# Decode attention with a gated feed-forward on one core: one part of the output-projection weights loaded as two DMAs, of 88 and of 40 partitions

## The chip, the core and the metric

The kernel runs on one core of a Trainium2 chip. The metric is the device time of one execution in microseconds. A time is given as the median of several executions. The profile is one execution of its own.

## What is computed

Two rows (batch 2, one new token each) of width 448 are normalised, and two branches are formed from them. Branch A is attention of 16 query heads over 8 key/value heads of width 256, for the last 2048 positions of a cache of 8192, and the output projection `wo`. Branch B is a two-layer feed-forward with a ReLU. The result is `x + A * silu(B)`.

```python
W = min(4096, max(256, Sk // 4))                       # 2048
q = (xn @ wq).reshape(B, Sq, Hq, Dh)                    # 2 x 1 x 16 x 256
scores = einsum("bhqd,bhkd->bhqk", q, k) * (Dh ** -0.5)
p = softmax(scores); o = einsum("bhqk,bhkd->bhqd", p, v)
s = o.reshape(B, Sq, Hq * Dh) @ wo                      # wo: 4096 x 448
g = silu(maximum(xn @ w1, 0) @ w2)
out = x + s * g
```

All inputs are bf16. The keys and values that are read are 32 MB, the weights about 10.5 MB, and `wo` alone 3.5 MB.

## The kernel before

The work is written as lists of operations, one list for each engine, with semaphore waits worked out from each operation's dependencies (`_Prog`, L24 to L159). The order on each engine is the order in which the operations are written.

Attention runs in four turns `u` = 0 to 3, each for one batch row and four key/value heads. A turn's keys (4 MB) go into one of two buffers `kbuf0` and `kbuf1`, its values (4 MB) into `vbuf0`, and the last turn's values into `vbuf1`. In a turn VectorE transposes the keys in four blocks (`do_T`, L376), TensorE forms the scores (`do_S`, L383), VectorE and ScalarE do the softmax (L400), and TensorE multiplies with the values (`do_PV`, L426). Then `attend_scale`, `attend_turn` and `attend_spread` (L443 to L467) bring the turn's result into `at_z`, from which the output projection reads it.

All large loads are issued by SyncE on its one queue, in the order in which they are needed: wq, keys 0, the rest of wq, keys 1, values 0, w1, w2, keys 2, values 1, keys 3, values 2, values 3 in two parts of 48 and 16 positions per partition (L566), and at last `wo` in seven parts. Each load has a semaphore of its own and counts as landed when 16 has been counted on it.

`wo` is laid out so that each of the 128 partitions holds 32 rows of 448 numbers (896 bytes each). A part of `n` rows per partition is one DMA with one piece of `n * 896` bytes for each partition. The parts are `WO_PARTS = [9, 7, 5, 4, 3, 2, 2]` (L191). They go into `kbuf0`, which is free when turn 2's scores are done (the dependency `st["S", 2, NBLK - 1]`). The loop that issues them is:

```python
for n in WO_PARTS:
    v, j = divmod(j0, NWO)
    d_wo[j0] = pr.dma(SP, wo_sb[:, j0 * D:(j0 + n) * D], wo_src[v, :, j * D:(j + n) * D], [st["S", 2, NBLK - 1]])
    j0 += n
```

The last turn ends on TensorE in this order (L574 to L610): a loop of five times two matmuls without use for the result (`idle_loop(5, 2)`, L574), the products with values 3 (the first three quarters wait for the first part of values 3, the last quarter for the second part), the spreading of turn 2's and turn 3's results, and the output projection `do_wo`. That is written in two pieces. Rows `j` = 0 to 8 (the first part of `wo`) are nine matmuls of 448 columns into `obk`. Their four column groups are added up by way of `sums` with eight more matmuls. Rows 9 to 31 are four matmuls of 112 columns each, 92 in all, into `hbk`. The first matmul of rows 9, 16, 21, 25, 28 and 30 waits for the part of `wo` that begins there (`d_wo.get(j)`, L590). After the 92 matmuls VectorE multiplies with the gate (L611), adds `x` (L613), and ScalarE issues the store of 8 x 112 numbers (L615).

Of the kernel before, what the change touches and what calls it, by code (L numbers as in the profile page):

```python
# [11 lines left out]
PE, DVE, ACTE, SP, POOL = "pe", "dve", "act", "sp", "pool"  # L12
# [149 lines left out]
def bass_recurrent_scan__sliding_block_cached__dense_activation_relu__decode_kernel(  # L162
# [11 lines left out]
    B, Sq, D = A_x.shape  # L174
# [11 lines left out]
    NBLK = DH // 64  # L186
# [6 lines left out]
    NWO = 16  # L193
# [5 lines left out]
    with es:  # L199
        pr = _Prog(nc, es)  # L200

        def named(name, shape, dt):
            return es.enter_context(nc.sbuf_tensor(name, shape, dt))
# [4 lines left out]
        def view(t, off, dims, n=128, p0=0, pstep=1):  # L208
            width = t.shape[1]
            return bass.AP(t, p0 * width + off, [[width * pstep, n]] + dims)  # L210
# [45 lines left out]
        at_z = named("at_z", [128, 32 * GAP], BF)  # L256
# [24 lines left out]
        wq_sb, w1_sb, w2_sb, wo_sb = vbuf[1], wf, wf, kbuf[0]  # L281
# [4 lines left out]
        wo_src = A_wo.rearrange("(v p j) n -> v p (j n)", v=2, j=NWO)  # L286
        assert SLOTS * HC <= UW and 32 * D <= UW and W2_AT + 14 * D <= UW

        st, d_k, d_v = {}, {}, {}
# [70 lines left out]
        def mm(out_ap, lhsT, rhs, start, stop=False, **kw):  # L360
            return lambda e: e.matmul(out_ap, lhsT=lhsT, rhs=rhs, start=start, stop=stop,  # L361
                                      skip_group_check=True, **kw)
# [134 lines left out]
        def tiled(bank, z, k, w, lo, first, last, deps):  # L497
            g = k % 4
            return pr.op(PE, mm(view(bank, 0, [[1, D]], n=2, p0=32 * g), view(z, k * GAP + 3, [[4, 2]]), w[:, lo:lo + D],
                                k < first, k >= last, tile_position=(0, 32 * g)), deps)  # L500
# [66 lines left out]
        d_wo, j0 = {}, 0  # L567
        for n in WO_PARTS:
            v, j = divmod(j0, NWO)
            d_wo[j0] = pr.dma(SP, wo_sb[:, j0 * D:(j0 + n) * D], wo_src[v, :, j * D:(j + n) * D], [st["S", 2, NBLK - 1]])  # L570
            j0 += n
        turn(3)
        v_f = pr.op(DVE, lambda e: e.tensor_copy(sums[:, :], view(fbk, 0, [[1, D]])), [st["F"]])
# [13 lines left out]
        def do_wo(lo, hi):  # L587
            o = None
            for j in range(lo, hi):
                deps = [d_wo.get(j), st["at_z", 2 + j // NWO]]  # L590
                if j < TILED:
                    o = tiled(obk, at_z, j, wo_sb, j * D, 4, TILED - 4, deps)
                    continue
                for i in range(4):
                    lo2 = j * D + i * NCOL
                    o = pr.op(PE, mm(view(hbk, 0, [[1, NCOL]], n=NROW), at_z[:, j * GAP + 3 - i:j * GAP + 3 - i + NROW],
                                     wo_sb[:, lo2:lo2 + NCOL], False, j == 2 * NWO - 1 and i == 3), deps)
                    deps = []
            return o

        attend_spread(3)
        m_t = do_wo(0, TILED)
        v_w = pr.op(DVE, lambda e: e.tensor_copy(sums[:, :], view(obk, 0, [[1, D]])), [m_t, m_f])
        idle_work(3)
# [3 lines left out]
        v_g = pr.op(DVE, lambda e: e.tensor_tensor(out=g_sb[:, :], in0=g_ap, in1=tmp[:, :], op=ALU.mult), [v_rc])  # L608
        fold_tiles(view(hbk, 0, [[1, NCOL]], n=NROW), True, False, [v_w])
        m_o = do_wo(TILED, 2 * NWO)  # L610
        v_t = pr.op(DVE, lambda e: e.tensor_tensor(  # L611
            out=tmp[:, :], in0=hbk[0:NROW, 0:NCOL], in1=g_sb[:, :], op=ALU.mult), [m_o, v_g])
# [33 lines left out]
```

## Time and profile before

| | us |
|---|---|
| time, median of 5 runs | 111.08 |
| lowest and highest of the 5 | 110.92 and 113.09 |
| time of the profiled execution | 112.69 |
| span in its profile | 111.2 |

The span is what lies between the first and the last instruction of the profile. The profiled execution's time is 1.49 us more than that. It is one execution, and it was 1.61 us longer than the median.

The DMA engines moved 44.13 MB in it, at a mean of 397 GB/s. VectorE was busy for 62.9 us and TensorE for 60.7 us.

A page gives busy time by engine, the span in 40 slices, the DMA queues, the chain of work that ended last, the costliest groups of instructions and the DMA issues. The trace also keeps for each load the sixteen times at which its semaphore was counted up by a DMA engine. Where such times are given, they are in us from the start of the span.

### The profile page before, as it was taken

What the parts mean: (1) busy time and instruction counts of PE and PEld (TensorE: products, weight loads), DVE (VectorE), ACT (ScalarE), POOL (GpSimd) and SP (SyncE); (2) the same over time, 40 slices, a digit from 0 to 9 for tenths busy, and PEclk for the clock granted to TensorE, in tenths of its full rate; (3) what the DMA queues carried; (4) which work ended last, traced back from release to release, by engine and by line L of the source; (5) the groups of instructions that cost most, each with busy time, mean ns of one, the idle gap of its engine ahead of it and who ended that gap; (6) DMA issues with size and microseconds to landing.
All of it is one profiled execution on the core that took longest, in us unless ns stands there. A gap on an engine that the chain in (4) does not pass through costs nothing. (4 is left out here: it accounts for less than half of the span.)

```text
span 111.2 us, 1362 instructions
## 1 busy us (share of the span) xinstructions
PE 60.7 (55%) x552; PEld 19.6 (18%) x558; DVE 62.9 (57%) x96; ACT 10.2 (9%) x19; POOL 3.1 (3%) x11
## 2 busy tenths in 40 slices
PE   0001000085699132999555788940078894798993
PEld 0000000030110020002141010220001033325692
DVE  1249009995200479992578998335699733615601
ACT  4990000000000200000200000020000002000000
POOL 7300000000000000000000000000000000000000
PEclk9999999999999975599985557999557999679999
DMA  3989989998998999999989999999999998999900
GB/s 65 490 383 495 448 351 464 482 401 377 530 412 377 424 419 392 415 447 542 401 365 436 460 412 389 495 412 412 448 448 424 395 433 383 420 414 407 376 25 1
DMA packets 3045, 44.13 MB, mean 397 GB/s; under 512 B 354, under 2 KB 612, under 8 KB 1508
## 3 DMA queue, kind: packets, MB, share of 16 engines
q1 hardware_dynamic: 3008, 44.11, 93.7%
q8 instruction: 1, 0.02, 0.1%
q10 hardware_dynamic: 36, 0.01, 0.0%
HBM read 44.11 MB, written 0.00 MB: 397 GB/s over the span
## 5 line engine op out<-in xcount | busy, mean ns | idle before, releaser
L379 DVE STREAM_TRANSPOSE kt<-kbuf 128x2048 f32<-128x2048 f32 x16 | 35.9, 2286 | 8.0 <-DMA kbuf<-in_A_k_cache_dram 8.0
L361 PE MATMUL sbk<-kt,qz 128*8 128x512 bf16 x128 | 31.0, 1070 | 13.7 <-PEq L102 13.6
L401 DVE TENSOR_REDUCE rm<-sbk 128x1 f32<-128x512 f32 x4 | 2.8, 691 | 14.5 <-PE sbk L361 14.5
L361 PE MATMUL obk<-vbuf,xr 128*4 128x512 bf16 x28 | 3.2, 627 | 13.9 <-DMA vbuf<-in_A_wq_dram 13.9
L407 ACT ACTIVATE et<-sbk,bias 128x512 bf16<-128x512 f32 x4 | 2.7, 687 | 81.1 <-DVE bias L405 81.1
L361 PEld LDWEIGHTS sbk<-kt,qz 128*8 128x8 bf16 x128 | 2.4, 87 | 29.1 <-issue 28.9
L361 PE MATMUL pbk<-et,spread 128*128 128x32 bf16 x64 | 2.6, 193 | 7.2 <-PEq L102 7.2
L361 PE MATMUL wbk<-q_n,ident 128*128 128x512 bf16 x9 | 4.5, 515 | 2.5 <-DVE qz L396 1.3
L361 PE MATMUL obk<-vbuf,pt 128*16 128x512 bf16 x96 | 5.8, 381 | 0.0
L361 PE MATMUL mbk<-ident,xg 2*128 2x2 bf16 x7 | 0.3, 163 | 8.5 <-DVE xg L325 8.5
L409 DVE STREAM_TRANSPOSE et<-et 128x512 bf16<-128x512 bf16 x4 | 2.8, 711 | 3.4 <-ACT et L407 3.4
L361 PE MATMUL hbk<-kbuf,at_z 128*8 128x112 bf16 x92 | 4.7, 213 | 0.0
L417 DVE TENSOR_TENSOR pt<-pbk,hmask 128x512 bf16<-128x512 f32 x4 | 2.8, 692 | 3.3 <-PE pbk L361 3.3
L361 PEld LDWEIGHTS hbk<-kbuf,at_z 128*8 128x8 bf16 x92 | 4.6, 87 | 0.0
L361 PEld LDWEIGHTS pbk<-et,spread 128*128 128x128 bf16 x64 | 2.2, 99 | 10.4 <-issue 10.4
L361 PEld LDWEIGHTS obk<-vbuf,pt 128*16 128x16 bf16 x96 | 2.5, 94 | 6.8 <-issue 4.7
L361 PEld LDWEIGHTS obk<-vbuf,xr 128*4 128x4 bf16 x28 | 0.8, 115 | 15.4 <-issue 15.4
L456 DVE TENSOR_TENSOR at_exp<-mbk,qmask 128x128 bf16<-128x128 f32 x4 | 1.2, 292 | 4.1 <-PE mbk L361 4.1
L611 DVE TENSOR_TENSOR tmp<-hbk,g_sb 8x112 f32<-8x112 f32 x1 | 0.3, 262 | 4.3 <-PE hbk L361 4.3
L361 PE MATMUL fbk<-wf,h_z 128*2 128x448 bf16 x14 | 1.7, 565 | 1.7 <-DVE h_z L494 1.7
L361 PE MATMUL obk_last<-vbuf,pt 128*16 128x512 bf16 x32 | 2.4, 400 | 0.0
L361 PEld LDWEIGHTS wbk<-q_n,ident 128*128 128x128 bf16 x15 | 1.5, 116 | 4.5 <-issue 2.2
(80 smaller groups left out, 44.8 us busy)
## 6 DMA issues: line engine op xcount, KB each, us to landing
kbuf<-in_A_k_cache_dram SPq DMA_DIRECT2D x4, 4096.0 KB, 23.5
vbuf<-in_A_v_cache_dram SPq DMA_DIRECT2D x3, 4096.0 KB, 15.8
wf<-in_B_w_dram SPq DMA_DIRECT2D x2, 1568.0 KB, 43.0
vbuf<-in_A_v_cache_dram SPq DMA_DIRECT2D x1, 3072.0 KB, 22.5
vbuf<-in_A_wq_dram SPq DMA_DIRECT2D x1, 2560.0 KB, 20.9
vbuf<-in_A_wq_dram SPq DMA_DIRECT2D x1, 1024.0 KB, 6.1
vbuf<-in_A_v_cache_dram SPq DMA_DIRECT2D x1, 1024.0 KB, 24.4
kbuf<-in_A_wo_dram SPq DMA_DIRECT2D x1, 1008.0 KB, 26.2
```

The lines of the kernel that those rows point to most:

```text
L361: return lambda e: e.matmul(out_ap, lhsT=lhsT, rhs=rhs, start=start, stop=stop, skip_group_check=True, **kw)
L379: st["kt", u, blk] = pr.op(DVE, lambda e: e.transpose(view(dst, 0, [[1, 32 * NT]]), view(src, 32 * blk, [[DH // 2, NT], [1, 32]])), [d_k[u ...
L401: v = pr.op(DVE, lambda e: e.tensor_reduce(out=rm[:, :], in_=sbk[:, :], axis=AX.X, op=ALU.max), [st["S", u, NBLK - 1]])
L407: a = st["exp", u] = pr.op(ACTE, lambda e: e.activation(e_sb, sbk[:, :], ACT.Exp, bias=bias[:, 0:1], accum_out=ssum[:, 0:1]), [v, st.get(( ...
L409: token = pr.op(DVE, lambda e: e.transpose(e_t, e_sb), [a, st.get(("Pt", u - 1))])
L417: st["pt", u] = pr.op(DVE, lambda e: e.tensor_tensor(out=view(pt, 0, [[8, NT], [2, 4], [1, 2]]), in0=view(pbk, 0, [[2, NT], [0, 4], [1, 2] ...
L456: st["at", u] = pr.op(DVE, lambda e: e.tensor_tensor(out=view(at_exp, 0, [[16, 8], [8, 2], [1, 8]]), in0=view(mbk, 136, [[1, 8], [8, 2], [ ...
L611: v_t = pr.op(DVE, lambda e: e.tensor_tensor(out=tmp[:, :], in0=hbk[0:NROW, 0:NCOL], in1=g_sb[:, :], op=ALU.mult), [m_o, v_g])
```

## The change

The part of three rows per partition (`n == 3`, rows 25 to 27) is issued as two DMAs, one after the other on the same queue: partitions 0 to 87, and partitions 88 to 127. [...]The bytes, their places and their place in the order of the queue are the same. Row 25's first matmul waits for both. All other parts are one DMA of 128 partitions as before.

```diff
         for n in WO_PARTS:
             v, j = divmod(j0, NWO)
-            d_wo[j0] = pr.dma(SP, wo_sb[:, j0 * D:(j0 + n) * D], wo_src[v, :, j * D:(j + n) * D], [st["S", 2, NBLK - 1]])
+            d_wo[j0] = []
+            for lo, hi in ((0, 88), (88, 128)) if n == 3 else ((0, 128),):
+                d_wo[j0].append(pr.dma(SP, wo_sb[lo:hi, j0 * D:(j0 + n) * D], wo_src[v, lo:hi, j * D:(j + n) * D],
+                                       [st["S", 2, NBLK - 1]]))
             j0 += n
...
             for j in range(lo, hi):
-                deps = [d_wo.get(j), st["at_z", 2 + j // NWO]]
+                deps = d_wo.get(j, []) + [st["at_z", 2 + j // NWO]]
```

## The prediction, made before the changed kernel ran

> **What bounds the kernel now.** I read the slices first, then the DMA issues, then the chain of waits, then the stages of its end.
>
> ```profile
> PEclk9999999999999975599985557999557999679999
> DMA  3989989998998999999989999999999998999900
> q1 hardware_dynamic: 3008, 44.11, 93.7%
> ```
>
> The DMA engines are busy from the second slice to about 106 us; one queue carries nearly all of it. So the last loads, `wo`, land when the stream ends, and only what follows their landing can be short or long. The query on DMA gives their sizes and the time from issue to landing:
>
> ```profile
> kbuf<-in_A_wo_dram SPq DMA_DIRECT2D x1, 1008.0 KB, 26.2
> ...
> kbuf<-in_A_wo_dram SPq DMA_DIRECT2D x2, 224.0 KB, 27.5
> kbuf<-in_A_wo_dram SPq DMA_DIRECT2D x1, 336.0 KB, 29.4
> ```
>
> The reader is to see that each waits over 25 us, in the queue behind values 2 and 3. The 336 KB part is the one that is changed. The chain of waits, from its last third:
>
> ```profile
> 97.68 0.63 PE wbk L361
> 98.32 1.12 PE obk_last L361 x16
> ...
> 102.55 0.66 PE obk L361 x9
> 103.21 0.16 issue
> 103.36 0.59 PE wbk L361 x2
> 103.96 5.43 PE hbk L361 x100
> 109.39 0.02 issue
> 109.42 0.27 DVE tmp L611
> ```
>
> No transfer stands in it: in this execution TensorE is late by itself. The reason is the clock in the stages (columns: stretch and length, PE, PEld, DVE, ACT and POOL busy, PEclk, DMA share, GB/s):
>
> ```profile
> 93.50:98.30 4.80, 3.71 (x27) 1.98 (x36) 1.94 (x4) 0.00 (x0) 0.00 (x0) 0.68 0.95 395
> 102.45:104.60 2.15, 1.99 (x20) 1.04 (x22) 1.55 (x4) 0.00 (x0) 0.00 (x0) 1.00 1.01 397
> 104.60:109.40 4.80, 4.78 (x95) 4.60 (x92) 0.52 (x2) 0.00 (x0) 0.00 (x0) 1.00 0.24 89
> ```
>
> The clock is half from 95.19 to 98.60 us, which falls on the loop of useless matmuls. Its five rounds of two begin at 94.73; the first took 0.43 us, each later one 0.85 or a little less. The value products follow at 98.32; at full clock the loop would end at 94.73 + 5 x 0.43 = 96.88, 1.44 earlier, and the 0.3 us of value products that fell in the half clock would give some 0.15 more: 1.59 in all. The execution was 1.61 above the median. So I read the median run as this one with TensorE about 1.6 earlier at its end, and there the landings matter.
>
> The trace's landing times, the last of sixteen for each part, and when its first matmul began here (92 matmuls in 104.69 to 109.38 start 0.049 apart, so row j begins at 104.69 + 4 x 0.049 x (j - 9)): row 0, landed 100.94, used 102.48; row 9, 102.88 and 104.69; row 16, 104.30 and 106.07; row 21, 105.42 and 107.05; row 25 (the changed part), 106.24 and 107.84; row 28, 106.82 and 108.43; row 30, 107.39 and 108.82. Each has 1.4 to 1.8 us of slack in this execution and next to none 1.6 us earlier. If only one part set the end, TensorE would end at its landing plus what followed its use here: row 0, 100.94 + 6.90 = 107.84; row 9, 107.57; row 16, 107.61; row 21, 107.75; row 25, 107.78; row 28, 107.77; row 30, 107.39 + 0.56 = 107.95. TensorE alone at full clock: 109.38 - 1.59 = 107.79. The profiled execution's own 112.69 has 3.31 us after 109.38; the median less this is 107.77. Four limits stand within 0.2 us of it.
>
> **What the Trainium skill says.** "DMA: Bandwidth & Descriptors", section "Why a DMA increments its semaphore by 16 and not by 1": a load issued by SyncE or ScalarE uses the largest count up to 16 that divides its partitions, the lowest-numbered ones, and the remaining counts are written at once. So 88 gives 11 and 40 gives 10. The trace agrees for 8: the load of `x_c` (8 partitions) shows one count at 1.78, standing for those written at once, and eight from 5.46 to 5.77. The same page, section "The descriptor swizzle", has a load of 128 partitions give each engine the rows of one SBUF port. "SBUF — State Buffer", section "Door 1: The DMA port swizzle", says that bandwidth depends on how many of the 16 ports are reached, and that partitions 0 to 63 reach 8 of them. Nothing in the trace of before has many bytes on fewer than 16 engines, so whether 11 engines keep their rate is unseen.
>
> **The change part by part.** Removed: 8 pieces of 2688 bytes from each of 16 engines. Added: 8 on engines 1 to 11 and 4 more on 1 to 10. Net: first ten +4, the eleventh 0, the last five -8. The price of one is from the distance of the last landings of rows 21 and 25: (106.24 - 105.42) / 8 = 0.103 us. So the first ten are later by 0.41 and the last five earlier by 0.82, from this part to the end of the queue.
>
> Whether that helps depends on who is last. The sixteen counts of row 30's part lie: eight from 105.82 to 105.99, seven from 106.10 to 106.83, one at 107.39. The same shape is in every load since keys 3, and the one straggler since the first: wq's first part has fifteen from 5.25 to 5.71 and one at 6.88. `x_c`, queued beside that part, was through on all of its eight engines by 5.77, so the straggler is not one of the first eight. Of the other eight, five are relieved, one is unchanged, two are burdened. I take it to be relieved. Then it counts at 107.39 - 0.82 = 106.57; the seven, if among the first ten, at most at 106.83 + 0.41 = 107.24. The last landing is between 106.57 and 107.24, so 0.15 to 0.82 earlier, for rows 28 and 30; row 25's two loads are both in by 106.09 at the latest.
>
> What it is worth: row 30's limit falls from 107.95 to 107.80 or below, and row 0's, 107.84, which the change doesn't touch, is next, with TensorE's own 107.79 behind it. Gain 107.95 - 107.84 = 0.11 us. In an execution like the profiled one the gain is 0.
>
> Other items. One more issue on SyncE: 0.43 us (the median of the `wo` issues), and two issues of the seven are held up by the queue (the last from 82.01 to 89.27). Behind it only the last two parts are issued, and even if the very last waited until the first part of values 3 has landed (95.99), its turn comes about 106, so it costs nothing; that cover of 10 us would have to go first. One more wait at row 25's first matmul: nothing stands between two instructions but the 0.02 to 0.05 us gaps of the chain, so 0 to 0.05, with 28 matmuls and the two VectorE operations behind it; hidden, since the two loads land before TensorE gets there. The other operations are the same in number and order on each engine. Sum on the profiled execution: 112.69 - 0.00; on the median: 111.08 - 0.11 = 110.97, so **111.0**.
>
> Unknown from both sides is the rate of the two loads. Below: at the rate of before, the above. Above: partitions 0 to 63 reach 8 ports, and if each engine takes 8 partitions in a row, engines 1 to 4 and 5 to 8 go to the same ports in pairs. Halved rate adds 0.82 for the load of 88 and 0 to 0.41 for that of 40: with the 0.41 of above, 1.23 to 1.64 on those engines. I take the lower value, since every other packet keeps its rate in this trace, and keep the upper for the range.
>
> **Rivals.** (1) Slower: the burdened engines become the last. Place: those of the first ten that are among the seven late ones; price: 1.23 to 1.64 by halved rate; it decides once the shift exceeds 107.39 - 106.83 = 0.56. Row 30 then lands at 106.83 + 1.23 = 108.06, up to 108.47: later by 0.67 to 1.08, so 111.75 to 112.16; I put 111.8. For it: the port rule above. Against: the eight early engines would have to shift by 1.40 before they matter. (2) Faster: row 30 alone sets the end in the unprofiled runs, and the limits of row 0 and of TensorE are lower there by more than I read. The gain is the landing's, up to 0.82; with 0.65 it is 110.4. For it: row 30's limit is the highest in my list. Against: the distance between row 0 and row 30 is set by one stream, and both shift together. (3) The straggler is the ninth or tenth engine: 107.39 + 0.41, so 111.08 + 0.41 = 111.5. (4) The split doesn't confine the loads to these engines: nothing changes, 111.1.
>
> **How the numbers follow.** The forecast 0.42, rival 3 0.10, rival 4 0.03: these lie within 0.5% (110.52 to 111.64), which is about what a measurement of this kernel can tell from no change. Rival 1 0.28, rival 2 0.17. So same 0.55, slower 0.28, faster 0.17. The range goes from 110.4, rival 2's value, to 111.9, which takes in the lower half of rival 1. The forecast's own range is 110.7 to 111.5.
>
> **What would show it.** Right: the straggler's counts of rows 25 to 31 come 0.4 to 0.8 earlier against those of row 21, and the chain of waits still has no transfer or has row 0's. Five counts of row 25's first load and six of its second come at once. Wrong: the distance from row 21's last landing to row 30's grows beyond 1.97 (107.39 - 105.42), or pieces of 2688 bytes that take well over 0.1 us (rival 1); an end that follows row 30's landing one for one (rival 2).

## The result, and the profile after

The changed kernel took 112.9 us (median of 42 runs). The kernel before, run beside it, took 111.67 us (79 runs, the five of the first table among them). The ratio is 1.0105, with a 95% interval of 1.0087 to 1.0123: slower by about 1.2 us.

The two profiled executions have spans of 110.8 us (after) and 111.2 us (before), and these can't be set against each other. In the one of before, the clock of TensorE was half during the loop of useless matmuls, in this one it was full. What can be compared is the order of events at the end. The slices of the changed kernel, TensorE's clock and the DMA engines:

```profile
PEclk9999999999999955579996569587555999999999
DMA  4989989998998999999999999899999999999960
```

The clock is full from slice 32 on. The DMA engines stay at nine tenths up to slice 38, as before; in slice 39 they are busy for six tenths, where before they were done. The issues, from the query on DMA:

```profile
kbuf<-in_A_wo_dram SPq DMA_DIRECT2D x1, 448.0 KB, 29.4
...
kbuf<-in_A_wo_dram SPq DMA_DIRECT2D x1, 231.0 KB
kbuf<-in_A_wo_dram SPq DMA_DIRECT2D x1, 105.0 KB
```

The 336 KB part has become two. The chain of waits of the changed kernel (start, length, what), from where it turns to a transfer:

```profile
77.17 29.42 DMA kbuf<-in_A_wo_dram
106.59 0.04 issue
106.63 2.34 PE hbk L361 x44
108.97 0.02 issue
109.00 0.27 DVE tmp L614
```

A transfer now stands in it. But it is not one of the two new loads. It was issued at 77.17 and has 44 matmuls behind it, so it is the 448 KB part, rows 21 to 24, which the change doesn't touch and which stands ahead of the new loads in the queue. The timeline of TensorE's last stage (start, length, engine, line, operation, tiles; in brackets the wait before it):

```profile
101.00 0.73 PE L361 MATMUL obk<-kbuf,at_z 128*2 128x448 bf16 x9
...
103.21 2.52 PE L361 MATMUL hbk<-kbuf,at_z 128*8 128x112 bf16 x48
...
106.63 2.33 PE L361 MATMUL hbk<-kbuf,at_z 128*8 128x112 bf16 x44 [0.90 <-DMA kbuf<-in_A_wo_dram]
```

The reader is to see that TensorE ran the 48 matmuls of rows 9 to 20 at its pace, and then stood for 0.90 us before row 21. The landing times (the last of all counts of a part, in us from the start of the span) tell where the delay begins. The last two lines are kernels of the experiments below: two loads of 64 partitions, and the part cut along its rows.

```
first row of the part     0       9      16      21      25      28      30
before                100.94  102.88  104.30  105.42  106.24  106.82  107.39
after                 100.95  102.88  104.54  106.59  107.14  107.61  108.18
halves                101.07  103.03  104.86  106.66  107.42  108.00  108.58
by rows, again        100.96  102.93  104.35  105.47  106.35  106.90  107.48
```

Up to row 9 before and after are alike within 0.01 us. Row 16 is 0.24 late, row 21 is 1.17 late, row 30 0.79. Row 21's last count comes at 106.59. All counts of the load of 88 partitions are in by 106.52. If an engine counts its loads in the order of the queue, which is assumed here, the engine that is last on row 21 takes no part in the load of 88: the straggler is one of the last five, and it was relieved, as the prediction took it. It was slowed before the relief came. In the trace's packet records the pieces of 3584 bytes (rows 21 to 24) took at most 0.155 us before and up to 0.309 after; those of 2688 bytes had a median of 0.107 us before and 0.165 after.

### The profile page after: what moved, and what is told of

It reads as the page before. It is cut to its first block, busy times and chain, and to the rows that moved or that the text cites. A ratio compares the mean times of both kernels' runs of the same rounds, so it can differ in the third digit from the quotient of the medians.

```text
span 110.8 us, 1364 instructions
## 1 busy us (share of the span) xinstructions
PE 60.9 (55%) x552; PEld 19.7 (18%) x558; DVE 62.9 (57%) x96; ACT 10.2 (9%) x19; POOL 3.1 (3%) x11
## 5 line engine op out<-in xcount | busy, mean ns | idle before, releaser
L361 PE MATMUL sbk<-kt,qz 128*8 128x512 bf16 x128 | 31.1, 1072 | 13.4 <-PEq L102 13.3
L361 PE MATMUL obk<-vbuf,pt 128*16 128x512 bf16 x96 | 6.6, 420 | 0.0
L361 PE MATMUL wbk<-q_n,ident 128*128 128x512 bf16 x9 | 3.5, 406 | 2.0 <-DVE qz L396 1.4
L444 DVE TENSOR_SCALAR o_sb<-obk,rs 128x512 bf16<-128x512 f32 x3 | 2.2, 730 | 0.0
```

The lines of the kernel that those rows point to most:

```text
L444: st["osb", u] = pr.op(DVE, lambda e: e.tensor_scalar(out=o_sb[:, :], in0=view(out_bank(u), 0, [[1, 512]]), scalar1=rs[:, u:u + 1], scalar ...
```

## The experiments

Theories at this point. *Shared ports*: a load that isn't one of 128 partitions gives each engine several partitions in a row. Two engines then write through one port of SBUF, the on-chip memory of 128 partitions, at a time, both at half rate, and an engine that is still on an earlier part is slowed through its own port too. *Burden*: the first ten engines have four pieces more, and that is all. *Issue and wait*: one more DMA on SyncE and one more wait on TensorE. *Reading side*: the order of the addresses in HBM, the memory that `wo` is read from.

**The split without partitions.** Two rows, then one row, of all 128 partitions.

```diff
-            for lo, hi in ((0, 88), (88, 128)) if n == 3 else ((0, 128),):
+            for a, b in ((0, 2), (2, 3)) if n == 3 else ((0, n),):
...
+                d_wo[j0].append(pr.dma(SP, wo_sb[:, (j0 + a) * D:(j0 + b) * D], wo_src[v, :, (j + a) * D:(j + b) * D],
+                                       [st["S", 2, NBLK - 1]]))
```

> Rows 25 to 27 as two loads of all 128 partitions, of two rows and of one, both waited for at row 25. Same extra issue on SyncE and same extra wait on TensorE as the changed kernel, no change in which engine or partition moves what. If the extra issue or the extra wait costs the time: ratio to before about 1.0105, like the changed kernel. If it is the partition split (shared ports, or more work on the first ten engines, or the reading side): 1.000, within 0.003, and the last landing of row 21's part stays about 1.1 us after row 16's.

Measured: ratio 0.9938 (0.9911 to 0.9966). Row 21's part landed 1.15 us after row 16's. The cost is gone. That it should be faster than before was not expected, so it was run again:

> The two loads of two rows and of one, once more, since the first look gave 0.9938 where 1.000 was expected and nothing in its landings tells why. If that was the luck of where the half-clock stretches fell: 1.000 within 0.004. If finer parts help in themselves: again 0.994.

Measured: 1.0012 (0.997 to 1.0055), so no change that can be told, and the first figure is no gain to rely on. Its landings stand in the table above and are those of the kernel before to 0.11 us. The extra issue and the extra wait cost nothing that shows. The clock was full in its profile from the loop on, as in that of the changed kernel, so these two can be set side by side. The end of its chain of waits:

```profile
75.57 25.39 DMA kbuf<-in_A_wo_dram
100.96 0.04 issue
101.00 0.73 PE obk L361 x9
...
108.12 0.27 DVE tmp L614
```

The last transfer in it is row 0's, and VectorE's multiplication starts at 108.12, where it started at 109.00 in the changed kernel: 0.88 us.

**The same work for every engine.** Two loads of 64 partitions, and two of 80 and 48. All of these counts are multiples of 16. These two kernels and the one with another source were run in the same rounds as the first run by rows, whose median was 111.67 us; theirs are 113.11, 112.73 and 112.91.

```diff
-            for lo, hi in ((0, 88), (88, 128)) if n == 3 else ((0, 128),):
+            for lo, hi in ((0, 64), (64, 128)) if n == 3 else ((0, 128),):
```

> Rows 25 to 27 as two loads of 64 partitions (0 to 63, 64 to 127). Each uses all 16 engines with 4 pieces, so every engine moves as much as before. Theory of shared ports (a load that is not of 128 partitions gives each engine partitions in a row, so that two engines write one port, and each slows whoever else is on that port): 64 partitions lie on 8 ports for 16 engines, pieces of 2688 bytes take about twice 0.107 us, row 21's straggler lands later than 1.1 us after row 16's, ratio 1.006 to 1.013. Theory of the burden (the first ten engines have 4 pieces more): nothing is left of it, ratio 1.000 within 0.003.

Measured: ratio 1.0074 (1.0042 to 1.0106). Each load counted sixteen times, so all engines took part. The median piece of 2688 bytes took 0.160 us, and row 21 landed 1.80 us after row 16 (1.12 before). The chain of waits of this kernel:

```profile
76.44 30.22 DMA kbuf<-in_A_wo_dram
106.66 0.04 issue
106.70 2.50 PE hbk L361 x44
```

It waits at the same place for the same untouched part, though nobody carries more than before.

> Rows 25 to 27 as two loads of 80 and of 48 partitions. Both use all 16 engines, with 5 and with 3 pieces, so every engine moves as much as before, but its partitions do not fall on the borders of ports. Shared ports: slower, ratio 1.004 to 1.013, pieces of 2688 bytes at a median well over 0.107 us. Burden: 1.000 within 0.003.

Measured: ratio 1.0045 (1.0007 to 1.0082), row 21 again 1.80 us after row 16, median piece 0.154 us. Both came as shared ports had it; burden alone can't do it. In both, row 16 landed 1.83 us after row 9 (1.42 before).

**Another source.** The split of 88 and 40, read from one packed stretch.

```diff
+        packed = A_wo[0:384, :].rearrange("(p j) n -> p (j n)", j=3)
...
+                src = wo_src[v, lo:hi, j * D:(j + n) * D] if n != 3 else packed[lo:hi, :]
```

> The split of 88 and 40 as in the changed kernel, but the source of both loads is one packed stretch of 344 KB of wo (the first 384 rows) and not every 32nd row; rows 25 to 27 of the projection are so left out and other rows taken in their place. The written side is the changed kernel's. If the reading side (the pattern of addresses in HBM) costs the time: ratio near 1.000. Shared ports or burden on the writing side: ratio about 1.010, as in the changed kernel, row 21's last landing 1.8 us or more after row 16's.

Measured: ratio 1.0071 (1.004 to 1.0102), row 21 landing 1.99 us after row 16. So the pattern of addresses that is read isn't the cause.

**The loads by themselves.** Seven loads one after the other behind the kernel before, with nothing else on the queue.

```diff
         pr.op(ACTE, None, [d_o])
+        last, N = d_o, NWO * D
+        for lo, hi in ((0, 128), (0, 88), (88, 128), (0, 64), (64, 128), (0, 80), (0, 128)):
+            last = pr.dma(SP, kbuf[1][lo:hi, 0:N], wo_src[0, lo:hi, :], [last])
+        pr.op(SP, None, [last])
```

> The kernel before, and after its output seven loads of wo rows by themselves, each issued when the one before has landed, 14336 bytes for each partition: 128 partitions, 0 to 87, 88 to 127, 0 to 63, 64 to 127, 0 to 79, 128 again. The added loads are no part of the computation; only their own landing times count. Shared ports with partitions in a row for each engine: 128 partitions take about [...]6.3 us; 64 partitions need the same time although each engine has half the pieces (4.3 us of transfer and not 2.1); 0 to 87 takes about twice the 4.3 us of its 8 pieces; 88 to 127 takes up to twice the 2.1 us of its 4. If every engine keeps its rate whatever the partitions (burden): 6.3, 6.3, 4.1, 4.1, 4.1, 4.7, 6.3.

The stages of the first six, from each load's first packet to the end of its last, in the order of the list (stretch and length, busy time by engine, clock, DMA share, GB/s):

```profile
111.37:117.36 5.99, 0.00 (x0) 0.00 (x0) 0.00 (x0) 0.00 (x0) 0.00 (x0) 0.53 0.81 306
118.63:127.32 8.69, 0.00 (x0) 0.00 (x0) 0.00 (x0) 0.00 (x0) 0.00 (x0) 0.50 0.64 144
128.98:133.38 4.40, 0.00 (x0) 0.00 (x0) 0.00 (x0) 0.00 (x0) 0.00 (x0) 0.50 0.57 130
135.26:139.79 4.53, 0.00 (x0) 0.00 (x0) 0.00 (x0) 0.00 (x0) 0.00 (x0) 0.50 0.93 203
141.87:146.45 4.58, 0.00 (x0) 0.00 (x0) 0.00 (x0) 0.00 (x0) 0.00 (x0) 0.50 0.91 197
148.19:153.52 5.33, 0.00 (x0) 0.00 (x0) 0.00 (x0) 0.00 (x0) 0.00 (x0) 0.50 0.91 215
```

The reader is to see that the load of 88 partitions needs 8.69 us for fewer bytes than the 128 partitions moved in 5.99, and that 64 partitions on all 16 engines move 203 and 197 GB/s instead of 306. By the packet records the median piece of 14336 bytes took 535 ns in the first load, 1087 in the load of 88, 1025 in that of 40, 1105 and 1131 in those of 64, and 1007 in that of 80. So a piece took 1.9 to 2.1 times as long in each of these loads, with nothing else on the queue. From one landing to the next the seven took 7.3, 10.4, 5.9, 6.6, 6.6, 7.0 and 7.4 us. A load of 128 took a microsecond more than was written down. A load of 64 took 0.7 us less than one of 128; burden had put it 2.2 us lower, and shared ports at the same time.

How many pairs of engines share a port doesn't explain all of this. If each engine takes partitions in a row, then by the prediction's own map of the ports engines 1 to 8 of the load of 88 are in pairs, and the other three, on partitions 64 to 87, have their ports to themselves. But its packets fall into eleven rows of eight, each packet beginning where one before it ended, and from the third piece on all eleven rows show 0.86 to 1.13 us for a piece. In the load of 80 all sixteen show 0.97 to 1.03 us from the third piece on, and the pairing gives no reason why they should be alike. Divided by the number of engines the rate is much the same in every load cut by partitions, 12.3 to 13.4 GB/s, against 19.1 with 128 partitions. So each engine of such a load is slowed, with or without a partner; why is open.

**Whose port.** Eight loads of 8 partitions each, four apart. They put the same bytes, in the same pieces, by the same first eight engines, either into the partitions that these engines write in a load of 128, or into those of the last eight engines. Which partitions these are follows the section on the swizzle that the prediction cites; no record here names an engine. The diff is that of the first; in the second the list is (64, 65, 66, 67, 96, 97, 98, 99).

```diff
-            d_wo[j0] = pr.dma(SP, wo_sb[:, j0 * D:(j0 + n) * D], wo_src[v, :, j * D:(j + n) * D], [st["S", 2, NBLK - 1]])
+            for p in (0, 1, 2, 3, 32, 33, 34, 35) if n == 3 else (None,):
+                dst, src = wo_sb[:, j0 * D:(j0 + n) * D], wo_src[v, :, j * D:(j + n) * D]
+                if p is not None:
+                    dst, src = wo_sb[p:p + 29:4, j0 * D:(j0 + n) * D], wo_src[v, p:p + 29:4, j * D:(j + n) * D]
```

> Rows 25 to 27 for partitions 0 to 63 alone, as eight loads of 8 partitions, four apart (0, 4, ..., 28; 1, 5, ...; up to 35, 39, ..., 63), so that each of the first eight engines writes the partitions it writes in a load of 128. Partitions 64 to 127 of these rows are not loaded and left out of the result. The last eight engines have 8 pieces less. Shared ports: nobody is slowed; pieces of 2688 bytes stay at about 0.107 us, row 21's last landing 1.1 us after row 16's, as before; ratio 0.994 to 1.003. Theory that any load of fewer partitions or on fewer engines is slow and holds up the others: as the run with other ports.

> The same eight loads as in the run with the engines' own ports, same bytes, pieces and engines, but for partitions 64 to 127 (64, 68, ..., 92; and so on), whose ports are those of the last eight engines; partitions 0 to 63 of rows 25 to 27 are left out of the result. Shared ports: the straggler among the last eight engines is still on rows 16 to 24 and is slowed: row 21's last landing 1.4 to 2.0 us after row 16's, pieces of 2688 bytes well over 0.107 us at the upper end; ratio 0.003 to 0.009 above that of the run with own ports. Otherwise both runs are alike.

Both kernels took much longer by the clock outside: 114.94 and 115.84 us, of which 4.7 and 4.8 us lie outside the span (1.5 in the kernel before). The ratio of the second is 1.0339 (1.0283 to 1.0395), and for the first, whose executions scatter from 111.87 to 116.87 us, none is given. The ratios that were written down were missed, and don't decide anything. So they are compared inside the span, where both profiled executions have the full clock at the end. TensorE's last stage with the engines' own ports:

```profile
101.03 0.73 PE L361 MATMUL obk<-kbuf,at_z 128*2 128x448 bf16 x9
...
103.25 4.69 PE L361 MATMUL hbk<-kbuf,at_z 128*8 128x112 bf16 x92
```

and with the other ports:

```profile
103.19 1.54 PE L361 MATMUL hbk<-kbuf,at_z 128*8 128x112 bf16 x28
104.92 1.15 PE L361 MATMUL hbk<-kbuf,at_z 128*8 128x112 bf16 x20 [0.20 <-DMA kbuf<-in_A_wo_dram]
106.26 2.33 PE L361 MATMUL hbk<-kbuf,at_z 128*8 128x112 bf16 x44 [0.19 <-DMA kbuf<-in_A_wo_dram]
```

With their own ports the 92 matmuls run without a stop from 103.25 to 107.94. With the other ports TensorE waits at row 16 and at row 21, and ends at 108.59, 0.65 later. Row 16 landed at 104.34 against 104.88, row 21 at 105.47 against 106.21. From row 9's landing to row 21's it is 2.53 us (2.54 before) against 3.36: 0.83 more, which is 8 pieces at 0.103 us, as if the straggler's port had to take the other engine's eight pieces in between. The pieces of 2688 bytes took 0.107 us against 0.189 at the median, and those of rows 21 to 24, which neither kernel changes, at most 0.155 against 0.292. The figure that was written down, row 21 at 1.4 us or more after row 16, was missed (1.33), because row 16 was already late; the delay began one part earlier than expected. So it matters to an engine that is still on an earlier part which partitions the others write. The last eight engines had rows 28 to 31 to write meanwhile, so these runs don't tell whether the eight pieces were slow because the port was in use, or because it was another engine's.

**The dose.** The split of 88 and 40 on the last part alone, and on rows 21 to 24 as well as 25 to 27.

```diff
-            for lo, hi in ((0, 88), (88, 128)) if n == 3 else ((0, 128),):
+            for lo, hi in ((0, 88), (88, 128)) if j0 == 30 else ((0, 128),):
```

> The split of 88 and 40 on the last part (rows 30 and 31, pieces of 1792 bytes) and none on rows 25 to 27. Shared ports: the same mechanism with two thirds of the bytes and one part later; row 21's last landing stays about 1.1 us after row 16's, row 28's moves to 0.8 us or more after row 25's (0.58 before), the last landing of all 107.4 or later; ratio 1.002 to 1.007. If only rows 25 to 27 matter because of where they stand: 1.000.

Measured: ratio 1.0022 (0.9987 to 1.0057), which doesn't tell it from no change. Row 28 landed 0.53 us after row 25, not 0.8 or more. The part that was hit is row 25's, 1.43 us after row 21's (0.82 before), two parts ahead of the new loads. The last landing of all, row 28's at 107.55, came as written down. In this profiled execution the half clock made TensorE late, as in that of before, and the delay doesn't reach its end.

```diff
-            for lo, hi in ((0, 88), (88, 128)) if n == 3 else ((0, 128),):
+            for lo, hi in ((0, 88), (88, 128)) if n in (3, 4) else ((0, 128),):
```

> The split of 88 and 40 on rows 21 to 24 (pieces of 3584 bytes) as well as on rows 25 to 27: the suspected cost 2.3 times over by bytes. Shared ports: row 16's last landing is now hit (1.8 us or more after row 9's, 1.42 before), the last landing of all is 108.8 or later, ratio 1.014 to 1.022. Relief of the straggler, if it were worth anything, would grow instead.

Measured: ratio 1.0287 (1.0226 to 1.0349), more than the upper end written down; part of it lies outside the span (a median of 2.2 us and not 1.5). Row 16 landed 2.95 us after row 9 (1.42 before), the last part at 110.17. The end of its chain of waits:

```profile
109.00 0.14 issue
109.14 1.64 PE hbk L361 x28
```

TensorE stands before row 25 until 109.00, when the second of that part's own two loads lands. More split bytes cost more; the relief of the straggler buys nothing.

## Why the prediction was wrong

**How the kernel of before is bound: right, as far as the profiles show.** The prediction read the median run as the profiled one with the loop at full clock, ending at 96.88, and several limits close together (in its own list more than the four that it counts). The changed kernel's profile has that clock: its first value product starts at 96.78, and it began row 0 at 101.00, just after its landing at 100.95.

**Engines, pieces, issue and wait: right.** The two new loads show one early count each, for those written at once, and then eleven and ten. The run with own ports relieved the straggler of 8 pieces without touching its port; row 30 landed at 106.56 and not 107.39, earlier by 0.83 where 0.82 was worked out. This gave TensorE nothing, since row 0's landing was next: it ended at 107.94, and 107.84 had been worked out for row 0's limit. The extra issue and wait were costed at nothing, and the runs by rows bear that out.

**The step that failed** is the rate of the two loads: "I take the lower value, since every other packet keeps its rate in this trace". That reason was none. Every other packet in that trace belongs to a load of 128 partitions (the two tiny loads of `x`, the store and the fetching of instructions apart), so the trace had nothing to say on a load of 88. The upper bound, half rate, is what was measured: 1087 against 535 ns at the median for the loads by themselves (in the stream of the changed kernel 0.165 against 0.107 us for the shorter pieces). The Trainium skill had a reason to expect it in "SBUF — State Buffer", section "Door 1: The DMA port swizzle", and in "DMA: Bandwidth & Descriptors", section "The descriptor swizzle", read together. It was in the text and was weighed too low. But pairs of engines on one port would have slowed eight of the eleven engines, and all eleven were slow: the bound was right, and its reason is not the whole one. The latter page's rule for the number of engines agrees with every load here (11 counts for 88 partitions, 10 for 40, 16 for 64 and 80), and these runs show that it isn't enough: with 64 or 80 partitions all 16 engines take part, and a piece takes about twice as long.

**A second step failed with it:** that the shift holds "from this part to the end of the queue" and leaves the parts ahead alone. Rival 1 took this over: it had the new loads slow, but the wrong victim. Its price put row 30 at 108.06 us, and it landed at 108.18. But the chain of waits is set by the straggler, whose count for row 21 came 0.57 us after the next engine's in the kernel of before. When the others begin the new loads it is still on rows 16 to 24, and is slowed there; the runs with own and other ports show such a slowing with the pieces and the number of engines equal. Row 21, untouched and ahead in the queue, is late by 1.17 us. Of this 0.88 us reach the end of TensorE's work, by comparison with the run by rows at the same clock. The medians differ by 1.2; they hold executions of both clocks, and the rest was not traced. Row 30 alone, at 108.18 + 0.56 = 108.74, would have cost nearly as much (the end was 108.97). One sign that was to show rival 1 came, the pieces of 2688 bytes at well over 0.1 us. The other, a growing distance from row 21's landing to row 30's, did not: it shrank from 1.97 to 1.59, since row 21 was late and the straggler was relieved after it. From row 16 it grows, from 3.09 to 3.64.

**The time.** 112.9 lies above the range, and above rival 1's 111.75 to 112.16. Of the distance to 111.0, 0.59 us is the median of before, which went from 111.08 to 111.67 with more runs; the rest is the slowdown, and the gain of 0.11 that didn't come.

## What to carry to other kernels

Before a load is cut by partitions, ask how fast its pieces will be, and not only how many engines it uses: with loads of 88, 40, 64 or 80 partitions a piece took about twice as long, where cutting along the row (two rows, then one) cost nothing that could be told. To give a late engine's rows to another gained nothing here: in the run with other ports the straggler became later by just the time of the eight pieces it was spared, and row 30 landed at 107.34 where it had landed at 107.39 before. And a change in a queue can hit the parts ahead of it, as long as one engine is still on them.

## What was not expected of the hardware

The kernels with eight loads of 8 partitions in place of one spent 4.7 and 4.8 us (medians) outside the span and not 1.5. One more load instead of seven more left it at 1.5; two more, in the run with two split parts, went with 2.2. Why was not tried.

The straggler is born in the first microseconds. In the trace of before, one packet of 16384 bytes on the queue for instructions took 0.92 us at 2.5 us, among the packets of wq's first part, and one engine's count for that part came at 6.88 where the fifteen others were done by 5.71. In every profile here one engine is last by 0.39 us or more when row 0's part lands. That this packet is the cause is argued from the times alone and wasn't tried.

That the thing shared is a port of SBUF is the skill's word for it. The runs with own and other ports show that the slowing of an engine ahead depends on which partitions the others write, with bytes, pieces and number of engines equal (the rows of `wo` that are read differ with the partitions). Which partitions each engine gets in a load of 88 or 64 was assumed and not seen.
